# Reordering the start of a fused attention and feed-forward kernel: batch 0 first, a fourth scratch set, a fourth staging place

## The chip, the cores and the metric

The kernel runs on one core of one Trainium2 chip. The metric is the device time of one execution in microseconds (us). Five engines work from queues of their own, each in order: TensorE (PE; its weight loads are listed as PEld), VectorE (DVE), ScalarE (ACT), GpSimd (POOL) and SyncE (SP), which here only issues DMAs.

## The reference, cut to what matters

```python
B, H, S, Ns, D = (4, 8, 512, 32, 64)

def _attn_ref(x, state):                       # x: B,H,S,D   state: B,H,Ns,D
    scale = 1.0 / np.sqrt(D)
    a  = softmax(scale * x @ state.T)          # over the 32 state rows, for each position
    xread = a @ state
    a2 = softmax(scale * state @ x.T)          # over the 512 positions, for each state row
    sread = a2 @ x
    return concat([xread, sread], axis=2)      # B, H, 512 + 32, D

def _moe_ref(x, w_in, w_out, alpha):           # 2176 tokens x 512; d_ff = 2048
    h = x @ w_in
    return (max(h, 0) + alpha * min(h, 0)) @ w_out

def _moe2_ref(x, w_in, w_out):
    h = x @ w_in
    return (max(h, 0) + log1p(exp(-abs(h)))) @ w_out

out = _moe2_ref(_moe_ref(attn as tokens x 512, ...), ...)
```

Both softmaxes subtract their maximum and add 1e-9 to their sum (written out in the code below). The four weight matrices are in double precision; the kernel turns each tile of them into single precision itself.

## The kernel before

The two feed-forward layers are `m = 0` and `m = 1`. Each is cut into four quarters `q` of 512 of the 2048 hidden columns. For each quarter the token blocks 0 to 3 (the 512 positions of a batch) and block `B` (the 128 state rows of all batches) are run through: `hidden` makes the hidden values of 128 columns (`fc`), `act` the activation and its split into a high and a low part (`g0h`, `g0l` and so on), and `out_part`, three jobs later (`LAG`), the second product, added up in `acc`. A block of positions has four jobs, block B has one; `n` counts the jobs of a quarter, 0 to 16. Each product of the layers is three matmuls on split values (`mm3`, L136 to L138): high by high, high by low, low by high.

In the first layer the attention's read is folded into the weights: the hidden value of a position is its softmax (`at`, from the row part of the attention) times the product of state and weights (`sw`, from `sw_batch`, L238). So hidden block 0 of a batch needs `at` and `sw` of this batch, and `sw` of a quarter needs its four tiles of `w_in`.

The attention works in eight groups `i` of four heads, two for each batch. For each group: `x` and `y` load it transposed (`xt`) and plain (`xs`); `s` makes the scores of state rows by positions (L269), copies them to SBUF (L270) and runs the softmax over positions (L271 to L275); `r` transposes the scores (L283) and runs the softmax over state rows (L286 to L292); `b` transposes this back and splits it into `at` (L299, L142, L145); `d` reads with the softmax over positions (L308 to L330) and leaves the state rows' tokens in `sr` for block B. Each group holds a scratch set of six 128x512 places; there are three sets, borrowed from places that are used later, taken in turn by `i % 3`.

A weight tile is loaded (`wload`) into one of three staging places of 4 KB a partition, converted (`wconv`: two ScalarE operations, L202 and L203, three VectorE operations, L204 to L206, and one sum on POOL, L207) and, except for `w_in` of the first layer, split (`wprep`: L142 on ScalarE, L145 on POOL). The intermediate tiles `top` and `exp` exist once. A conversion asks for the next load when it is done. Tiles are converted at most four ahead of what is prepared.

The order of the start is written out by hand: `LOADS` (first DMAs), `BEFORE` (ahead of the first hidden block) and `AMONG` (ahead of job `n` of the first quarter). A letter is a step and its digit the group: `L` load of a weight tile, `p` prepare one (convert it if need be, then split), `c` convert one, `w` the state products of a batch, and the letters above. This is the order of the program; when the kernel is built, a scheduler sets the order on each engine, which may put a later step first where an earlier one is not ready by its own reckoning. PSUM has two pools of four banks, `psa` (state products, hidden blocks, most of the attention) and `psb` (output parts, and some of the first groups).

Of the kernel before, what the change touches and what calls it, by code (L numbers as in the profile page):

```python
# [8 lines left out]
F32 = mybir.dt.float32  # L9
F32R = mybir.dt.float32r  # L10
BF16 = mybir.dt.bfloat16
U16 = mybir.dt.uint16
# [6 lines left out]
P = 128  # L19
# [25 lines left out]

LOADS = "L0 x0 L0 y0 x1 L0 x2 y2 y1"
BEFORE = "p0 s0 c0 s1 r0 p0 c0 r1 d0 b0 p0 x3 d1 y3 p0 w0 b1 p0 y4 s2 p0 r2 c0 x4 s3 w1 c0"
AMONG = ("d2 r3 b2", "d3 s4 x5", "b3", "r4", "s5 y5 p0 d4 x6", "p0 r5 s6", "y6 d5 r6 b4 b5", "", "y7 x7 s7 d6", "b6 r7", "d7 b7")

SPLIT_FIRST = (9, 10, 11, 12, 13, 14, 15, 16)  # L50
SPLIT = (1, 2, 4, 5, 7, 9, 10, 16)
# [7 lines left out]
def mixer_kernel(  # L59
# [26 lines left out]
    class Place:  # L86
# [11 lines left out]
        r = property(lambda self: self.get(F32R))  # L98

    def sbp(name):  # L100
        return Place(name + "h"), Place(name + "l")
# [20 lines left out]
    g_p = pairs(4, "g")  # L122
    acc = [Place(f"acc{i}") for i in range(17)]
    stg = [sbt([P, W], I64, f"stg{i}") for i in range(3)]
    cnv = [sbt([P, W], F32, f"cnv{i}") for i in range(4)]
    tmp = [sbt([P, W], F32, f"tmp{i}") for i in range(3)]
# [5 lines left out]
    st_s = [sbt([P, 16], F32, f"sts{i}") for i in range(2)]  # L132
    st_n = [sbt([P, 2], F32, f"stn{i}") for i in range(3)]

# [46 lines left out]
    def is_whole(i):  # L181
        return wsrc[i][:2] == ("i", 0)

    def wload():
        i = nload[0]
        if i < len(wsrc):
            to, of = stg[i % len(stg)].bitcast(U16), wsrc[i][4].bitcast(U16)
            nc.sync.dma_start(out=to[:, 0 : 4 * W - 1], in_=of[:, 1 : 4 * W])
            nload[0] += 1

    def wconv():

        i = nconv[0]
        if i >= len(wsrc) or i >= nprep[0] + len(cnv):
            return
        s = stg[i % len(stg)]
        top = s.bitcast(U16).rearrange("p (n t) -> p n t", t=4)[:, :, 2]
        low = s.bitcast(U32).rearrange("p (n t) -> p n t", t=2)[:, :, 0]
        a = take_place(i).f if is_whole(i) else cnv[i % len(cnv)]
        t, e = (x[i % len(x)] for x in top_t)  # L200
        tu, eu = t.bitcast(U16), e.bitcast(U16)
        nc.scalar.activation(e, top.bitcast(BF16), AF.Abs)  # L202
        nc.scalar.activation(tu, eu, AF.Relu, bias=top_bias, scale=TOP_SCALE)  # L203
        nc.vector.scalar_tensor_tensor(out=tu, in0=top, scalar=TOP_SIGN, in1=tu, op0=ALU.bitwise_and, op1=ALU.bitwise_or)  # L204
        nc.vector.tensor_scalar(eu, tu, TOP_EXP, None, op0=ALU.bitwise_and)  # L205
        nc.vector.scalar_tensor_tensor(out=a, in0=low, scalar=REST, in1=e, op0=ALU.mult, op1=ALU.mult)  # L206
        nc.gpsimd.tensor_tensor(out=a, in0=t, in1=a, op=ALU.add)  # L207
        wload()
        nconv[0] += 1
# [35 lines left out]
    NG = 2 * B  # L245
    sets = [acc[8:14], flat(wo_p[4:7]), acc[14:17] + [wi_p[4][0], wi_p[4][1], at_p[7][1]]]

    def at_load_t(i):
# [7 lines left out]
    def scratch(i):  # L256
        for x in sets[i % 3]:
            held.pop(x.name, None)
        return [x.f for x in sets[i % 3]]

    def at_scores(i):

        b, g = i // 2, i % 2
        t, n2 = scratch(i), st_n[i % 3]
        ps = bank(pool_s(i))
# [4 lines left out]
        nc.scalar.activation(t[4], ps, AF.Copy)  # L270
        nc.vector.tensor_reduce(out=n2[:, 0:1], in_=ps, op=ALU.max, axis=AX.X)  # L271
        nc.vector.tensor_scalar(n2[:, 0:1], n2[:, 0:1], -SCALE, None, op0=ALU.mult)
        nc.scalar.activation(t[5], ps, AF.Exp, bias=n2[:, 0:1], scale=SCALE, accum_out=n2[:, 1:2])
        nc.vector.tensor_scalar(n2[:, 1:2], n2[:, 1:2], EPS, None, op0=ALU.add)
        nc.vector.reciprocal(n2[:, 1:2], n2[:, 1:2])  # L275

    def at_rows(i):
# [11 lines left out]
        nc.vector.tensor_reduce(out=s1, in_=e3, op=ALU.add, axis=AX.X)  # L289
        nc.vector.tensor_scalar(s1, s1, EPS, None, op0=ALU.add)  # L290
        nc.vector.reciprocal(s1, s1)
# [10 lines left out]
    def at_read(i):  # L302

        b, g = i // 2, i % 2
        t, n2 = scratch(i), st_n[i % 3]
        ps = bank(pool_s(i))
# [145 lines left out]
    def at_do(what):  # L452
        for x in what.split():
            i = int(x[1:])
            if x[0] == "s":
                at_scores(i)
            elif x[0] == "r":
                at_rows(i)
# [29 lines left out]
    for m in range(2):  # L488
        for q in range(NQ):
            first = m == 0 and q == 0  # L490
            blocks = (0, 1, 2, B, 3) if first else (0, 1, B, 2, 3)
            n = 0
            for b in blocks:
                for fc in range(4 if b < B else 1):
# [9 lines left out]
                    todo.append((m, q, b, fc, g))  # L504
                    wconv()
                    if m == 0:
                        if n in SW_AHEAD and q < NQ - 1:
                            sw_batch(q + 1, SW_AHEAD.index(n))
                        if first and b in (0, 1) and fc == 2:
                            sw_batch(q, b + 2)  # L510
                        if not first and n == SW_LAST:
                            sw_batch(q, B - 1)
                    if n in (SPLIT_FIRST if first else SPLIT):
                        wprep()
# [39 lines left out]
```

## Time and profile before

| | us |
|---|---|
| median of 3 runs | 753.28 |
| lowest, highest | 752.79, 753.40 |
| the profiled execution | 752.3 |
| its span, from the first to the last instruction | 750.5 |
| busy: TensorE, VectorE, ScalarE, POOL | 727.6, 425.3, 423.2, 170.5 |
| mean granted clock of TensorE | 0.995 |

Busy TensorE means that a matmul is in its pipeline by the profile's model of its end; neighbouring matmuls overlap, so that busy time is no measure of pace. The granted clock is 1.00 at 2.4 GHz and 0.50 at 1.2 GHz. Idle time in brackets names what ended it.

### The profile page before, as it was taken

The numbers are of one execution on the slowest core, as the hardware profiler recorded it, in microseconds if no ns is written. First come the engines' busy times: TensorE is split into PE (matmuls) and PEld (weight loads), VectorE is DVE, ScalarE is ACT, GpSimd is POOL, SyncE is SP. The second block draws the span as 40 slices with busy tenths as digits, with TensorE's granted clock in tenths as the row PEclk, the third lists the DMA queues.
The fourth block names the chain that finished last, engine by engine and source line by source line (L and its number), as shares of the span: only waits on it lengthen the run. The fifth ranks groups of instructions, "written<-read, shape, count | busy, mean of one in ns | idle before, by whom it ended". The sixth has DMA issues, their size and how long they took to land.

```text
span 750.5 us, 9504 instructions
## 1 busy us (share of the span) xinstructions
PE 727.6 (97%) x3580; PEld 561.7 (75%) x3580; DVE 425.3 (57%) x693; ACT 423.2 (56%) x764; POOL 170.5 (23%) x142
## 2 busy tenths in 40 slices
PE   5699998999999999999999999999999999999998
PEld 2267665777777777878888888888888888888886
DVE  4898657757778447885575224654257342333433
ACT  4778767735554335554677647755466354444560
POOL 2352332402142003452571003410044000000000
PEclk9989999999999999999999999999999999999999
DMA  9654313203211001220122001220010000001102
GB/s 323 221 174 156 107 44 115 85 7 108 83 57 57 0 1 58 86 82 1 56 79 91 0 1 57 84 85 1 0 57 0 1 1 0 1 1 56 57 15 112
DMA packets 16654, 47.27 MB, mean 63 GB/s; under 512 B 2016, under 2 KB 2016, under 8 KB 16608
## 3 DMA queue, kind: packets, MB, share of 16 engines
q1 hardware_dynamic: 16608, 46.66, 18.4%
q8 instruction: 28, 0.46, 0.3%
q14 instruction: 18, 0.15, 0.1%
HBM read 42.20 MB, written 4.46 MB: 62 GB/s over the span
## 4 chain that ended last, share of the span: by engine, by line
PE 94%; DVE 2%; ACT 2%; DMA 1%; issue 1%; POOL 0%; SPq 0%; ACTq 0%
PE pb L136 17%; PE pb L138 17%; PE pb L137 17%; PE pa L136 13%; PE pa L137 12%; PE pa L138 12%; PE pa L238 2%; PE pa L359 2%; PE pa L269 1%; DMA acc<-xt 1%; DVE top L204 1%; PE pa L367 0%; ACT exp L202 0%; PE pb L269 0%; ACT top L203 0%
## 5 line engine op out<-in xcount | busy, mean ns | idle before, releaser
L386 DVE SCALAR_TENSOR_TENSOR pa<-pa,tmp 128x512 f32<-128x512 f32 x68 | 47.4, 697 | 128.8 <-ACT tmp L385 128.8
L383 ACT ACTIVATE tmp<-pa 128x512 f32<-128x512 f32 x68 | 40.5, 596 | 92.7 <-PE pa L138 73.0
L429 DVE TENSOR_TENSOR acc<-pb,acc 128x512 f32<-128x512 f32 x102 | 67.4, 686 | 37.4 <-PE pb L138 37.4
L204 DVE SCALAR_TENSOR_TENSOR top<-stg,top 128x512 uint16<-128x512 uint16 x64 | 53.0, 828 | 46.8 <-ACT top L203 46.2
L207 POOL TENSOR_TENSOR cnv<-top,cnv 128x512 f32<-128x512 bf16 x48 | 56.4, 1175 | 101.0 <-DVE cnv L206 97.2
L379 DVE SCALAR_TENSOR_TENSOR pa<-tmp,rest,pa 128x512 f32<-128x512 f32 (+1 forms) x80 | 53.2, 671 | 25.7 <-ACT tmp L375 25.2
L202 ACT ACTIVATE exp<-stg 128x512 bf16<-128x512 bf16 x64 | 42.9, 671 | 38.7 <-DVE cnv L206 28.6
L375 ACT ACTIVATE tmp<-pa 128x512 f32<-128x512 f32 x68 | 40.2, 596 | 43.0 <-PE pa L138 36.4
L203 ACT ACTIVATE top<-exp,top_bias 128x512 uint16<-128x512 uint16 x64 | 46.1, 721 | 9.2 <-POOL cnv L207 5.5
L385 ACT ACTIVATE tmp<-tmp 128x512 f32<-128x512 f32 x68 | 42.9, 630 | 1.7
L384 ACT ACTIVATE tmp<-tmp 128x512 f32<-128x512 f32 x68 | 42.9, 631 | 1.5
L206 DVE SCALAR_TENSOR_TENSOR cnv<-stg,exp 128x512 f32<-128x512 uint32 x48 | 35.8, 745 | 13.0 <-POOL wo5l L145 4.1
L205 DVE TENSOR_SCALAR exp<-top 128x512 uint16<-128x512 uint16 x64 | 32.1, 502 | 1.1
L142 ACT ACTIVATE g1h<-pa 128x512 fp32r<-128x512 f32 x33 | 19.7, 596 | 20.8 <-DVE pa L386 12.4
L142 ACT ACTIVATE g3h<-pa 128x512 fp32r<-128x512 f32 x33 | 19.7, 596 | 19.3 <-DVE pa L379 9.6
L142 ACT ACTIVATE g0h<-pa 128x512 fp32r<-128x512 f32 x33 | 19.6, 594 | 19.1 <-DVE pa L379 10.2
L145 DVE TENSOR_TENSOR g3l<-pa,g3h 128x512 fp32r<-128x512 f32 x33 | 22.7, 689 | 13.4 <-ACT g3h L142 13.2
L145 DVE TENSOR_TENSOR g1l<-pa,g1h 128x512 fp32r<-128x512 f32 x33 | 22.7, 688 | 12.7 <-ACT g1h L142 12.3
L145 DVE TENSOR_TENSOR g0l<-pa,g0h 128x512 fp32r<-128x512 f32 x33 | 22.7, 688 | 10.5 <-ACT g0h L142 10.1
L145 DVE TENSOR_TENSOR g2l<-pa,g2h 128x512 fp32r<-128x512 f32 x33 | 22.7, 687 | 10.0 <-ACT g2h L142 9.9
L142 ACT ACTIVATE g2h<-pa 128x512 fp32r<-128x512 f32 x33 | 19.7, 597 | 14.5 <-DVE pa L386 7.6
L145 POOL TENSOR_TENSOR wo3l<-cnv,wo3h 128x512 fp32r<-128x512 f32 x5 | 6.5, 1294 | 76.1 <-ACT wo3h L142 75.9
(863 smaller groups left out, 2119.7 us busy)
## 6 DMA issues: line engine op xcount, KB each, us to landing
stg<-w1i SPq DMA_DIRECT2D x16, 511.8 KB, 4.0
stg<-w1o SPq DMA_DIRECT2D x16, 511.8 KB, 3.4
stg<-w2i SPq DMA_DIRECT2D x16, 511.8 KB, 3.9
stg<-w2o SPq DMA_DIRECT2D x16, 511.8 KB, 3.3
out<-acc SPq DMA_DIRECT2D x16, 256.0 KB, 2.0
acc<-xt SPq DMA_DIRECT2D x10, 256.0 KB, 4.8
acc<-xs SPq DMA_DIRECT2D x8, 256.0 KB, 5.3
wo4h<-xt SPq DMA_DIRECT2D x3, 256.0 KB, 3.5
```

Source lines behind the costliest of these rows:

```text
L136: nc.tensor.matmul(ps, lh, rh, start=start, stop=False)
L137: nc.tensor.matmul(ps, lh, rl, start=False, stop=False)
L138: nc.tensor.matmul(ps, ll, rh, start=False, stop=stop)
L142: nc.scalar.activation(h, src, AF.Copy)
L145: eng_l.tensor_tensor(out=l, in0=src, in1=h, op=ALU.subtract)
L202: nc.scalar.activation(e, top.bitcast(BF16), AF.Abs)
L203: nc.scalar.activation(tu, eu, AF.Relu, bias=top_bias, scale=TOP_SCALE)
L204: nc.vector.scalar_tensor_tensor(out=tu, in0=top, scalar=TOP_SIGN, in1=tu, op0=ALU.bitwise_and, op1=ALU.bitwise_or)
L207: nc.gpsimd.tensor_tensor(out=a, in0=t, in1=a, op=ALU.add)
L379: nc.vector.scalar_tensor_tensor(out=ps[:, cs], in0=t[:, cs], scalar=a, in1=ps[:, cs], op0=ALU.mult, op1=ALU.add)
L386: nc.vector.scalar_tensor_tensor(out=ps, in0=ps, scalar=0.0, in1=t, op0=ALU.max, op1=ALU.add)
L429: nc.vector.tensor_tensor(out=a, in0=ps, in1=a, op=ALU.add)
```

## The change

The order lists are written anew: the four `w_in` tiles and both groups of batch 0 go first; other groups, the conversions of `w_out` and batch 1's state products come after them. The position softmax is a step of its own (`e`, `at_positions`), which reads the scores' copy in SBUF in place of PSUM and comes later than the scores. Three operations on one or 16 values a partition go from VectorE to POOL. There are four scratch sets (`i % 4`) and four places for the position softmax's maximum and sum. The fourth weight tile has a staging place of its own, which later holds `acc0` and `acc1` (`Half`). In the first quarter block B comes last, conversions stop at 16 tiles, the state products of batches 2 and 3 move from jobs 2 and 6 to jobs 5 and 9, and one preparation moves from the first quarter to the second (`SPLIT_SECOND`).

```diff
-LOADS = "L0 x0 L0 y0 x1 L0 x2 y2 y1"
-BEFORE = "p0 s0 c0 s1 r0 p0 c0 r1 d0 b0 p0 x3 d1 y3 p0 w0 b1 p0 y4 s2 p0 r2 c0 x4 s3 w1 c0"
-AMONG = ("d2 r3 b2", "d3 s4 x5", "b3", "r4", "s5 y5 p0 d4 x6", "p0 r5 s6", "y6 d5 r6 b4 b5", "", "y7 x7 s7 d6", "b6 r7", "d7 b7")
-SPLIT_FIRST = (9, 10, 11, 12, 13, 14, 15, 16)
+LOADS = "L0 x0 L0 x1 L0 L0 y0"
+BEFORE = "p0 s0 p0 s1 r0 p0 r1 x2 y1 p0 b0 w0 b1 x3 y2 y3"
+AMONG = (
+    "e0 d0 s2 p0", "r2 s3 e1 d1 p0", "r3 b2 p0", "b3 w1 p0 x4 y4",
+    "e2 d2 x5 y5", "s4 r4 e3 d3", "s5 r5 b4 x6 y6", "b5 e4 d4 x7 y7",
+    "e5 d5 s6 r6", "s7 r7 b6 e6", "d6 b7", "e7 d7",
+)
+SPLIT_FIRST = (9, 10, 11, 12, 13, 14, 15)
+SPLIT_SECOND = (2, 3, 4, 5, 7, 9, 10, 12, 16)
...
-    acc = [Place(f"acc{i}") for i in range(17)]
+    acc01 = {"name": "acc01"}
+    acc = [Half(acc01, 0), Half(acc01, 1)] + [Place(f"acc{i}") for i in range(2, 17)]
+    stg_3 = sbt([P, W], I64, acc01["name"])
...
-    st_n = [sbt([P, 2], F32, f"stn{i}") for i in range(3)]
+    st_n = [sbt([P, 2], F32, f"stn{i}") for i in range(4)]
...
+    def stage(i):
+        return stg_3 if i == 3 else stg[(i - (i > 3)) % len(stg)]
...
-        wload()
+        if i != 3:
+            wload()
...
+    sets.append([ex_p[0][1], ex_p[1][0], ex_p[1][1], wi_p[5][0], wi_p[5][1], sr[1]])
...
         nc.scalar.activation(t[4], ps, AF.Copy)
-        nc.vector.tensor_reduce(out=n2[:, 0:1], in_=ps, op=ALU.max, axis=AX.X)
-        nc.vector.tensor_scalar(n2[:, 0:1], n2[:, 0:1], -SCALE, None, op0=ALU.mult)
-        nc.scalar.activation(t[5], ps, AF.Exp, bias=n2[:, 0:1], scale=SCALE, accum_out=n2[:, 1:2])
-        nc.vector.tensor_scalar(n2[:, 1:2], n2[:, 1:2], EPS, None, op0=ALU.add)
+
+    def at_positions(i):
+
+        t, n2 = scratch(i), st_n[i % len(st_n)]
+        nc.vector.tensor_reduce(out=n2[:, 0:1], in_=t[4], op=ALU.max, axis=AX.X)
+        nc.gpsimd.tensor_scalar(n2[:, 0:1], n2[:, 0:1], -SCALE, None, op0=ALU.mult)
+        nc.scalar.activation(t[5], t[4], AF.Exp, bias=n2[:, 0:1], scale=SCALE, accum_out=n2[:, 1:2])
+        nc.gpsimd.tensor_scalar(n2[:, 1:2], n2[:, 1:2], EPS, None, op0=ALU.add)
         nc.vector.reciprocal(n2[:, 1:2], n2[:, 1:2])
...
-        nc.vector.tensor_scalar(s1, s1, EPS, None, op0=ALU.add)
+        nc.gpsimd.tensor_scalar(s1, s1, EPS, None, op0=ALU.add)
...
-            blocks = (0, 1, 2, B, 3) if first else (0, 1, B, 2, 3)
+            blocks = (0, 1, 2, 3, B) if first else (0, 1, B, 2, 3)
...
-                    wconv()
+                    if not first or nconv[0] < 4 * NQ:
+                        wconv()
...
-                        if first and b in (0, 1) and fc == 2:
-                            sw_batch(q, b + 2)
+                        if first and n in (5, 9):
+                            sw_batch(q, 2 + (n == 9))
...
-                    if n in (SPLIT_FIRST if first else SPLIT):
+                    if n in (SPLIT_FIRST if first else SPLIT_SECOND if (m, q) == (0, 1) else SPLIT):
```

## Rows read from the trace of the kernel before

**Rows 1.** The page: busy us (share of the span) and instructions of TensorE.
```profile
PE 727.6 (97%) x3580; PEld 561.7 (75%) x3580; DVE 425.3 (57%) x693; ACT 423.2 (56%) x764; POOL 170.5 (23%) x142
```
**Rows 2.** Windows: stretch, its length, busy by engine, granted clock, DMA share, GB/s.
```profile
7.27:35.42 28.15, 19.88 (x166) 7.40 (x167) 22.65 (x51) 18.96 (x44) 9.71 (x9) 0.98 0.80 291
35.42:41.70 6.28, 6.28 (x50) 3.75 (x50) 6.16 (x14) 4.78 (x11) 3.32 (x3) 0.53 0.37 126
41.70:125.00 83.30, 79.66 (x557) 54.70 (x554) 63.25 (x124) 61.84 (x137) 28.33 (x24) 1.00 0.36 118
...
160.00:200.00 40.00, 40.00 (x193) 29.71 (x192) 30.28 (x54) 21.69 (x36) 8.22 (x7) 1.00 0.29 93
```
**Rows 3.** The chain that ended last: start us, us, engine, tile, line.
```profile
34.69 0.68 DVE sw2l L145
35.44 0.78 PE pa L136
...
42.90 0.23 PE pa L137
...
55.90 0.99 PE pa L269 x8
...
58.26 0.44 PE pa L308 x4
...
70.85 0.58 PE pa L314 x32
...
108.25 3.43 PE pa L359 x8
```
**Rows 4.** Windows of 1 us: length, busy TensorE, granted clock, DMA share, GB/s.
```profile
31.00:32.00 1.00, 0.00 (x0) 1.00 0.82 305
...
35.00:36.00 1.00, 0.58 (x1) 0.50 0.19 41
...
42.00:43.00 1.00, 1.00 (x6) 1.00 0.62 174
```
**Rows 5.** Timeline, end of the first quarter: start, us, instruction [idle before].
```profile
121.49 0.50 PE L136 MATMUL pa<-at6h,sw6h 128*128 128x512 f32 x1 [2.37 <-DVE g1l L145]
```
**Rows 6.** Timeline: fourth weight tile's load and conversion's end, batch 0's last input.
```profile
13.25 0.33 SPq L188 DMA_DIRECT2D stg<-w1i  x1
...
24.75 1.16 POOL L207 TENSOR_TENSOR wi1l<-top,wi1l 128x512 f32<-128x512 bf16 x1 [2.15 <-DVE wi1l L206]
...
30.27 0.69 DVE L145 TENSOR_TENSOR sw1l<-pa,sw1h 128x512 fp32r<-128x512 f32 x1 [0.44 <-ACT sw1h L142]
```
**Rows 7.** Timeline: the first weight tile's conversion.
```profile
6.69 0.72 ACT L203 ACTIVATE top<-exp,top_bias 128x512 uint16<-128x512 uint16 x1
...
7.44 0.69 DVE L204 SCALAR_TENSOR_TENSOR top<-stg,top 128x512 uint16<-128x512 uint16 x1 [6.58 <-ACT top L203]
...
9.27 1.16 POOL L207 TENSOR_TENSOR wi0h<-top,wi0h 128x512 f32<-128x512 bf16 x1 [7.97 <-DVE wi0h L206]
```
**Rows 8.** Timeline: the first and the last of the four output tiles' conversions.
```profile
28.52 1.17 POOL L207 TENSOR_TENSOR cnv<-top,cnv 128x512 f32<-128x512 bf16 x1 [2.61 <-DVE cnv L206]
...
47.79 1.18 POOL L207 TENSOR_TENSOR cnv<-top,cnv 128x512 f32<-128x512 bf16 x1 [1.49 <-DVE cnv L206]
```
**Rows 9.** Timeline: group 7 from its row transposes to `at7l`; block 3's first product.
```profile
92.25 0.60 PE L283 MATMUL pa<-ident,wo6h 128*128 128x128 f32 x4
...
103.67 0.69 DVE L145 TENSOR_TENSOR at7l<-pa,at7h 128x512 fp32r<-128x512 f32 x1 [4.67 <-ACT at7h L142]
...
116.45 0.48 PE L136 MATMUL pa<-at6h,sw6h 128*128 128x512 f32 x1
```
**Rows 10.** Timeline: POOL's nearest small operation; a product and a 16-bit operation beside it.
```profile
1.01 0.29 POOL masks.py:199 TENSOR_SCALAR_AFFINE_SELECT ident<-ident 128x128 f32<-128x128 f32 x1
...
21.54 1.05 POOL L292 TENSOR_TENSOR wo4l<-wo4l,sts 128x512 f32<-128x512 f32 x1 [0.49 <-DVE sts L291]
21.84 1.30 DVE L204 SCALAR_TENSOR_TENSOR top<-stg,top 128x512 uint16<-128x512 uint16 x1 [0.47 <-ACT top L203]
```

More of the change, by code (lines that the diff above doesn't have):

```diff
@@ L98, in mixer_kernel, with __init__, f @@
         r = property(lambda self: self.get(F32R))
+    class Half:
+        def __init__(self, both, k):
+            self.name, self.both, self.k = f"{both['name']}{k}", both, k
+        @property
+        def f(self):
+            if "f" not in self.both:
+                self.both["f"] = sbt([P, 2 * W], F32, self.both["name"])
+            return self.both["f"][:, self.k * W : (self.k + 1) * W]
     def sbp(name):
@@ L186, in wload @@
         if i < len(wsrc):
-            to, of = stg[i % len(stg)].bitcast(U16), wsrc[i][4].bitcast(U16)
+            to, of = stage(i).bitcast(U16), wsrc[i][4].bitcast(U16)
             nc.sync.dma_start(out=to[:, 0 : 4 * W - 1], in_=of[:, 1 : 4 * W])
@@ L195, in wconv @@
             return
-        s = stg[i % len(stg)]
+        s = stage(i)
         top = s.bitcast(U16).rearrange("p (n t) -> p n t", t=4)[:, :, 2]
@@ L256, in scratch @@
     def scratch(i):
-        for x in sets[i % 3]:
+        for x in sets[i % len(sets)]:
             held.pop(x.name, None)
-        return [x.f for x in sets[i % 3]]
+        return [x.f for x in sets[i % len(sets)]]
     def at_scores(i):
         b, g = i // 2, i % 2
-        t, n2 = scratch(i), st_n[i % 3]
+        t = scratch(i)
         ps = bank(pool_s(i))
@@ L304, in at_read @@
         b, g = i // 2, i % 2
-        t, n2 = scratch(i), st_n[i % 3]
+        t, n2 = scratch(i), st_n[i % len(st_n)]
         ps = bank(pool_s(i))
@@ L456, in at_do @@
                 at_scores(i)
+            elif x[0] == "e":
+                at_positions(i)
             elif x[0] == "r":
```

## The prediction

> **What bounds the kernel now.** I read the page first: TensorE is busy 97% of the span [rows 1]. Then the busy time by stage [rows 2]: from 41.7 us on TensorE is nearly full, and in the stretch of 160 to 200 us it is full while VectorE has a quarter and ScalarE almost half of the time free. So no change off TensorE can help there, and only the start is open. TensorE's first matmul is at 7.27 us, when the first transposed group has landed; its first matmul of the feed-forward part (L136) is at 35.42. Between the two it counts as busy for 19.88 of 28.15 us, but a busy TensorE is not TensorE at its pace, so I price the work instead, with the chain's rows at full clock [rows 3]: a set of score or state products (eight 64x512) 0.99, four transposes 0.44, the 32 small products of a read 0.58, one 128x512 product 0.23. Issued in that stretch: scores of four groups 3.96, four row transposes 1.76, two whole reads (0.44 + 0.58 + a quarter of 0.44 = 1.13) 2.26 and the transposes of a third 0.44, two back transposes 0.88, state weights of two batches 3.96: 13.3 us. So 14.9 of the 28.15 us are lost.
>
> After this comes a stretch at the lower clock: the granted clock falls to 0.50, that is 1.2 GHz, after TensorE had done little for some microseconds, and is back at 1.00 (2.4 GHz) by 42 us [rows 4]. From 35.42 to 41.70 it did six products, one set of transposes, the small products of one read and one score set: 1.38 + 0.44 + 0.58 + 0.99 = 3.4 us of work in 6.28, so 2.9 lost. Later there is one visible hole, 2.37 us before 121.49, where a hidden block waits for a PSUM bank that g1l gives free [rows 5]. The losses that the change can reach are thus 14.9 + 2.9 + 2.4 = 20.2 us.
>
> Why does the feed-forward start so late? Batch 0's last input, sw1l, is done at 30.27 + 0.69 = 30.96 [rows 6], and the chain of waits then shows the first hidden block waiting for sw2l, done at 35.37 [rows 3]: that is batch 1's state product, made ahead of hidden block 0, and it held a bank of the pool of four that the hidden blocks use. VectorE is busy 22.65 of the 28.15 us [rows 2], and its queue is in order.
>
> **The change part by part.**
>
> *Loads.* Before, the fourth weight tile is issued at 13.25, since its staging place has to be read first [rows 6]. After, it has a place of its own and goes out with the first three, ahead of x2, y2 and y1; x1 goes ahead of y0. The queue's bytes up to there are nearly the same, so the first matmul stays at 7.27. No cost.
>
> *Weights of batch 0.* The first conversion ends at 9.27 + 1.16 = 10.43 [rows 7]; the fourth ends at 24.75 + 1.16 = 25.91 [rows 6], so the next three take (25.91 - 10.43)/3 = 5.2 each. The bound from below: the next tile's L203 must wait until POOL has read `top`, so a period is L203 0.72, then VectorE's three from 7.44 until POOL starts at 9.27 (1.83), then POOL 1.16, and two hops of about 0.05: 3.8. What lies between 3.8 and 5.2 is other work on ScalarE and VectorE: the position softmax of groups 0 and 1 (moved to e0, e1), and s2, r2 and batch 1's part, which the new order puts behind. Four tiles then end between 10.43 + 3 x 3.8 = 21.8 and 25.9; I take 23.9, the middle, because the row softmax of groups 0 and 1 still shares the engines. The last state products (half a set, 0.5), the copy (0.6), the subtraction (0.69) and hops and queue waits of 1.3 follow: batch 0 is ready at 27 (24.5 to 31).
>
> *Work before that.* Of TensorE's work, scores of groups 0 to 3 (groups 2 and 3 wait on no earlier group now that there are four scratch sets), three row transposes, two back transposes, one state batch and one read fit ahead: 3.96 + 1.32 + 0.88 + 1.98 + 1.13 = 9.3 us. Lost: 27 - 7.27 - 9.3 = 10.4 instead of 14.9, **gain 4.4** (0 if batch 0 is no earlier than 31, 6.9 at 24.5). Hidden block 0 no longer stands behind batch 1's state product, and a score bank is free after its copy, because the position softmax reads the copy in SBUF.
>
> *Low clock.* TensorE will again have a sparse stretch before 27 us, but with more work in it. Before, the fall came only after the nearly empty stretch up to 35. I take half: **gain 1.4** (0 to 2.9).
>
> *Feeding it after 27 us.* The output weights come one by one: before, the four tiles are converted from 29.69 to 48.97, 6.4 us apart [rows 8]. After, TensorE has from 27 us hidden blocks 0 to 3 (24 products, 5.5), their output parts (48 products, 11.0) and s4, r3, b2, b3, d1, w1 (5.4): 21.9 us. If the first output tile is done at 28, the others 5.2 apart, and the fourth split 2.5 later, it is ready at 46: 19 us for 21.9 us of work. In sum there is enough; but each queue is in order, so some waits will show: **loss 1.5** (0, up to 3 x (6.4 - 2.8) = 10.8 if nothing stands between the output parts of 2.8 us each).
>
> *Conversions capped at 16 in the first quarter*, where 20 fitted: 4 x 1.8 = 7 us of VectorE go to the second quarter and lie under TensorE there (9.7 us free of 40 [rows 2]). Without that cover it would be up to 7 us. The one preparation more in the second quarter has the same cover.
>
> *State rows' block last.* Its work is the same, so nothing by itself. It takes distance from batch 3: group 7's row transposes at 92.25 lead to at7l at 104.36, and block 3 starts at 116.45 [rows 9], 12.1 us of slack. The state block (3.43 [rows 3], 0.44 and 12 x 0.23: 6.6) and one place (18 x 0.23 = 4.1) go: 1.4 us remain. On the other side the 2.37 us hole came where the state block, batch 3 and two state products shared four banks. I take half of it: **gain 1.2** (from 2.4 to a loss of 2).
>
> *Small operations to POOL*, three a group, 24 in all. No row has one there; the nearest is 0.29 for 128x128 [rows 10], the far bounds nothing and the 1.05 of a 512-wide product. VectorE is spared 24 x 0.15 = 3.6. On batch 0's path lies the one in the row softmax, hidden under the weights' chain, which ends later; without this cover it is 0.3 plus a wait behind one POOL operation, 1.2. I take 0. But VectorE's 16-bit L204 takes 1.30 instead of 0.69 while POOL's product runs from 21.54 to 22.59 [rows 7, 10].
>
> The Trainium skill, "SBUF — State Buffer", section "Who interferes with whom", says that the two engines share one port pair, which whichever starts first holds for the whole instruction while the other is blocked. The trace's 1.30 against 0.69 agrees. By that rule each moved operation is a new hold on VectorE, and the sum would be about 1.8 us worse; by the rows alone it is not.
>
> Sum: -4.4 - 1.4 + 1.5 - 1.2 = -5.5. The profiled execution took 752.3 (span 750.5 and 1.8 around it), so 746.8 on its own scale; the median shown is 1.0 higher, so **747.8 us**.
>
> **The rivals.**
>
> *All of it is kept.* Batch 0 at 24.5, full clock throughout, no waits: -6.9 - 2.9 - 2.4 = -12.2, 741.1. For it: the arithmetic of 21.9 us of work against 19. Against: VectorE near full up to 41.7. Chance 0.17 for below 744.
>
> *Blocked VectorE.* Six moved operations come before 27 us (one each in r0 and r1, two each in e0 and e1), each holding VectorE for 0.3: batch 0 at 28.8, 749.6. The 1.30 row speaks for it, 0.15 spared per operation against. Chance 0.10.
>
> *No earlier.* The order on each engine is made when the kernel is built; if it puts s2, s3 and r2 in front of batch 0's work on VectorE, or banks run out again, batch 0 stays at 31 and the first output tiles are as late as before: 752 to 754. Chance 0.18. The change would then not do what it says.
>
> *Slower: output parts wait in TensorE's queue.* Place: between hidden block 3 and batch 1's hidden blocks. If tiles still come 6.4 us apart and output parts stand in line ahead of everything else, 10.8 is lost against 7.0 gained: 756.6 + 1.0 = 757.1 or so on the median's scale. It decides from 2.3 us of wait per tile, a period of 5.1. For it: before, the period was 6.4 with VectorE full; against: before, TensorE found other work. Chance 0.15.
>
> **How the numbers follow.** The forecast's own case, 744 to 751.5, has 0.40. A measurement of this kernel tells about 0.2% (1.5 us) from no change. Faster: 0.40 + 0.17 + 0.10 = 0.67; within 0.2%: 0.18; slower: 0.15. The range runs from 741.5 (under it 0.02) to 755 (over it 0.15).
>
> **What would show it.** Right: L136's first matmul at 25 to 28 us, its waits there naming sw1l and not sw2l; the fourth weight tile converted by 24; the first score of group 3 before 22; less than 2.9 us lost at clock 0.50; TensorE full between 30 and 48; no wait before batch 3's blocks. Wrong: first L136 past 30; waits of TensorE on output tiles (wo1 to wo3) of over 2 us each between 30 and 48; a wait on at7 or at6 at batch 3; or L204 and L205 often above 1 us.

## The result, and the profile after

The changed kernel takes 758.6 us (median of six runs, 756.28 to 759.72), the kernel before, run beside it, 753.22 (751.86 to 753.83): ratio 1.0071, interval 1.0055 to 1.0087. It is slower by 5.4 us where 5.5 less was forecast, and outside the range. The profiled execution took 756.28, the lowest of the six, so profiles show 4.0 of it.

First the page's busy time, then the windows that answer to those of before; the last two lines are windows from 40 us.

```profile
PE 729.2 (97%) x3580; PEld 562.8 (75%) x3580; DVE 424.0 (56%) x669; ACT 424.7 (56%) x764; POOL 177.1 (23%) x166
```
```profile
7.27:35.42 28.15, 22.92 (x159) 10.63 (x156) 22.45 (x44) 19.58 (x41) 12.97 (x19) 0.94 0.80 297
35.42:41.70 6.28, 3.66 (x15) 2.82 (x14) 6.28 (x13) 4.85 (x14) 3.58 (x5) 0.83 0.73 217
41.70:125.00 83.30, 76.31 (x582) 50.78 (x581) 52.79 (x92) 57.09 (x126) 26.68 (x32) 0.99 0.28 89
...
40.00:60.00 20.00, 18.04 (x92) 12.54 (x90) 12.60 (x21) 12.11 (x22) 8.49 (x8) 0.93 0.44 137
60.00:105.00 45.00, 39.97 (x334) 27.24 (x335) 33.42 (x62) 34.11 (x79) 18.46 (x25) 1.00 0.33 106
```

Against [rows 2], TensorE is busier up to 35.42 (22.92 for 19.88 us), but from there to 125 it is busy 3.66 + 76.31 = 79.97 us where before it was 6.28 + 79.66 = 85.94. VectorE is not short from 41.70 on: 52.79 for 63.25. The kernel before, in the same windows from 40 us:

```profile
40.00:60.00 20.00, 20.00 (x142) 12.44 (x134) 19.20 (x35) 14.64 (x35) 8.92 (x8) 0.97 0.58 185
60.00:105.00 45.00, 43.73 (x351) 30.87 (x349) 31.58 (x66) 33.03 (x77) 13.85 (x12) 1.00 0.32 106
```

TensorE's queue waits for answers more often: 9 waits from 20 to 140 us, 13.1 us in sum, where before there were 7 with 10.0, and only two of those behind 40 us. First the waits after the change, from 20 to 140 us, then the two of before from 40 to 140 us (who waits, for whom, us in total, times, longest):

```profile
PE pb L327 <- POOL acc L320: 2.6, 1, 2.6
PE pa L311 <- ACT wi5l L294: 2.4, 1, 2.4
PE pa L261 <- POOL wi1l L229: 2.2, 1, 2.2
PE pb L155 <- ACT g3h L161: 1.9, 1, 1.9
PE pa L155 <- DVE acc L315: 1.4, 1, 1.4
PE pa L342 <- ACT wo6h L337: 1.2, 1, 1.2
...
```
```profile
PE pa L136 <- DVE g1l L145: 2.4, 1, 2.4
PE pa L136 <- ACT srh L330: 1.2, 1, 1.2
```

L327 is the back transpose of group 2, L311 the row transposes of group 7, L155 a 128x512 product, L342 the small products of a read. The tiles wo6h, wi4l and wi5l in these waits are places that the groups borrow as scratch, not weights. From the timeline, in order: the start of e0 on VectorE, the last step of the fourth weight tile's conversion, the first hidden product, the last step of the first and of the last output tile's conversion, and the output part that waits for g3h.

```profile
9.97 0.69 DVE L299 TENSOR_REDUCE stn<-acc 128x1 f32<-128x512 f32 x1 [1.02 <-ACT acc L294]
...
24.23 1.16 POOL L229 TENSOR_TENSOR wi1l<-top,wi1l 128x512 f32<-128x512 bf16 x1
...
27.44 0.80 PE L155 MATMUL pa<-at0h,sw0h 128*128 128x512 f32 x1
...
29.24 1.17 POOL L229 TENSOR_TENSOR cnv<-top,cnv 128x512 f32<-128x512 bf16 x1 [1.19 <-DVE cnv L228]
...
46.82 1.17 POOL L229 TENSOR_TENSOR cnv<-top,cnv 128x512 f32<-128x512 bf16 x1 [1.68 <-DVE cnv L228]
...
54.76 1.20 PE L155 MATMUL pb<-g3h,wo3h 128*128 128x512 f32 x4 [1.90 <-ACT g3h L161]
```

The start did what was forecast: batch 0's hidden product at 27.44 instead of 35.42 [rows 3]. To see what became of it I priced all of TensorE's work up to an instant at the prediction's prices (the 128x512 product by 0.2275, a quarter of a transpose set by 0.109, a matmul of the state block's L387 by 3.43 / 8 = 0.4286). An instant less the work started by then is an estimate of what TensorE has **lost** by it, in us; the last columns are runs told of below.

```
instant  before  after   e13    e14    e11    e12
  7.27     7.1    7.0    7.0    7.0    7.0    7.0
 27.44    17.5   18.5   19.0   17.8   18.9   17.8
 35.42    22.2   21.5   21.5   22.2   21.8   21.1
 50       26.1   25.2   25.4   27.1   22.7   23.2
 80       27.7   30.0   31.9   30.5   29.2   24.5
105       28.9   34.9   33.0   32.7   32.3   25.8
130       32.3   35.9   33.5   36.9   32.9   29.5
735       28.9   33.0   30.9   34.6   30.2   26.6
```

The changed kernel is 1.0 behind at 27.44, ahead by only 0.7 at 35.42 and 0.9 at 50, loses 3.2 more than before from 50 to 80, 3.7 more from 80 to 105, gains 2.4 from 105 to 130 and gives 0.5 back behind it: +4.1, the difference of the two profiles.

### The profile page after: what moved, and what is told of

It reads as the page before. It is cut to its first block, busy times and chain, and to the rows that moved or that the text cites. A ratio compares the mean times of both kernels' runs of the same rounds, so it can differ in the third digit from the quotient of the medians.

```text
span 754.5 us, 9484 instructions
## 1 busy us (share of the span) xinstructions
PE 729.2 (97%) x3580; PEld 562.8 (75%) x3580; DVE 424.0 (56%) x669; ACT 424.7 (56%) x764; POOL 177.1 (23%) x166
## 4 chain that ended last, share of the span: by engine, by line
PE 90%; DVE 3%; ACT 3%; POOL 1%; issue 1%; DMA 1%; SPq 0%
PE pb L155 16%; PE pb L156 16%; PE pb L157 16%; PE pa L155 12%; PE pa L157 12%; PE pa L156 12%; PE pa L261 3%; PE pa L387 2%; DVE top L226 1%; ACT top L225 1%; DMA acc<-xt 1%; POOL cnv L229 0%; PE pa L395 0%; PE pa L311 0%; PE pb L293 0%
## 5 line engine op out<-in xcount | busy, mean ns | idle before, releaser
L226 DVE SCALAR_TENSOR_TENSOR top<-stg,top 128x512 uint16<-128x512 uint16 x63 | 52.6, 834 | 51.9 <-ACT top L225 51.4
L164 DVE TENSOR_TENSOR g3l<-pa,g3h 128x512 fp32r<-128x512 f32 x33 | 22.7, 689 | 12.8 <-ACT g3h L161 12.5
L164 DVE TENSOR_TENSOR g0l<-pa,g0h 128x512 fp32r<-128x512 f32 x33 | 22.7, 688 | 10.8 <-ACT g0h L161 10.4
L164 DVE TENSOR_TENSOR g2l<-pa,g2h 128x512 fp32r<-128x512 f32 x33 | 22.7, 688 | 10.2 <-ACT g2h L161 10.0
L164 DVE TENSOR_TENSOR g1l<-pa,g1h 128x512 fp32r<-128x512 f32 x33 | 22.7, 687 | 10.3 <-ACT g1h L161 9.9
```

Of the source, the lines that this page charges most:

```text
L164: eng_l.tensor_tensor(out=l, in0=src, in1=h, op=ALU.subtract)
```

## The experiments

Each ratio is to runs of the kernel before on the same chip. e1 to e4 ran on one chip, e5 to e8 on a second, e9 to e12 on a third, e13 to e16 on a fourth; e17 and e18 stand beside runs of their own.

**First ideas: the steps on POOL, the block order, the places, batch 1.**

e1_small_on_vector:
```diff
-nc.gpsimd.tensor_scalar(n2[:, 0:1], n2[:, 0:1], -SCALE, None, op0=ALU.mult)
+nc.vector.tensor_scalar(n2[:, 0:1], n2[:, 0:1], -SCALE, None, op0=ALU.mult)
...
-nc.gpsimd.tensor_scalar(s1, s1, EPS, None, op0=ALU.add)
+nc.vector.tensor_scalar(s1, s1, EPS, None, op0=ALU.add)
```


> The changed kernel with its three small operations a group back on VectorE; all else as changed. Theory 'late batch 1' (the order puts batch 1's steps behind block 0, so that TensorE runs out of work between 50 and 65 us): VectorE gets 3.6 us back and POOL's hops go, but block 1 still starts near 60; 757 to 759. Theory 'POOL' (the small operations wait behind POOL's long ones and lengthen each row softmax): the hole before b2 (2.6 us at 36.7) and those at 83 to 95 us shrink, 753 to 755.

759.51 us, 1.0092 (1.0077 to 1.0107): no gain. The operations on POOL are not the cause.

e2_state_block_fourth:
```diff
-blocks = (0, 1, 2, 3, B) if first else (0, 1, B, 2, 3)
+blocks = (0, 1, 2, B, 3) if first else (0, 1, B, 2, 3)
```


> The changed kernel with the state rows' block back between blocks 2 and 3 of the first quarter; all else as changed. Theory 'late batch 1': the loss lies before 65 us and at 92, where nothing changes; 757 to 760. Theory 'state block' (its place costs the slack of the last groups): 754 to 756, with the hole before 95.0 gone or moved.

762.08 us, 1.0124 (1.0109 to 1.0139): the state block's place last saves about 0.5%, some 4 us, in the changed kernel.

e3_before_with_places (the kernel before with the fourth places and one more early weight load):
```diff
-LOADS = "L0 x0 L0 y0 x1 L0 x2 y2 y1"
+LOADS = "L0 x0 L0 y0 x1 L0 L0 x2 y2 y1"
...
+    sets.append([ex_p[0][1], ex_p[1][0], ex_p[1][1], wi_p[5][0], wi_p[5][1], sr[1]])
...
+    def stage(i):
+        return stg_3 if i == 3 else stg[(i - (i > 3)) % len(stg)]
```


> The kernel before with the new places alone: four scratch sets, the fourth staging place (one more load among the first), four places for maximum and sum; its order lists, its position softmax, its conversions and its block order unchanged. Theory 'late batch 1' (the order costs, the places do not): no slower than before, 751 to 754. Theory 'places' (more loads at once and other borrowed places cost): 755 or more.

755.78 us, 1.0043 (1.0026 to 1.006): there the places cost 3 us. e10 below shows that they are not what the changed order pays for.

e4_batch1_ahead:
```diff
-BEFORE = "p0 s0 p0 s1 r0 p0 r1 x2 y1 p0 b0 w0 b1 x3 y2 y3"
+BEFORE = "p0 s0 p0 s1 r0 p0 r1 x2 y1 p0 b0 w0 b1 x3 y2 y3 s2 r2 s3 w1"
 AMONG = (
-    "e0 d0 s2 p0", "r2 s3 e1 d1 p0", "r3 b2 p0", "b3 w1 p0 x4 y4",
+    "e0 d0 r3 b2 p0", "e1 d1 b3 p0", "p0", "p0 x4 y4",
```


> The changed kernel with batch 1's steps moved forward: s2 r2 s3 w1 to the end of BEFORE, r3 b2 to job 0 and b3 to job 1; all else as changed. Theory 'late batch 1': block 0 starts some us later than 27, but block 1 starts before 57 and the loss between 40 and 65 us shrinks from 8 to about 4; 752 to 755. Theories 'POOL' and 'state block': no better than the changed kernel, 757 to 760.

758.07 us, 1.0069 (1.0054 to 1.0084): the same as the changed kernel. The edit did not bring block 1 forward: it starts at 61.0 (60.72 without the edit), while block 0's first hidden product falls back to 31.6. The wait of group 2's back transposes shrinks from 2.6 to 1.2 and that for g3h goes, so batch 1's steps gain by it what the start loses. Moving them is no gain in sum; what they cost where the change has them stays open. The run also shows that 4 us of the earlier start can be given up without a loss.

**Conversions and queue order.**

e5_two_intermediates, and e8_before_two_intermediates with the same edit on the kernel before:
```diff
+    pair2 = sbt([P, 2 * W], BF16, "acc4")
...
         t, e = (x[i % len(x)] for x in top_t)
+        if i % 2 and i < 10:
+            t, e = pair2[:, 0:W], pair2[:, W : 2 * W]
```


> The changed kernel, with a second pair of the two intermediate tiles for every other output tile among the first ten. In the changed kernel's trace the output tiles' conversions end 5.9 us apart on average between 29.24 and 46.82 us, VectorE is busy for only 17.18 of the 24.58 us from 35.42 to 60, and its output weights are whole only at about 50 us. Conversion-chain theory: one pair of intermediates makes the tiles' steps on POOL, ScalarE and VectorE follow each other, and this sets the pace from 27 to 50 us; with two pairs the tiles come 4 to 5 us apart, the last of the first four some 4 us earlier, block 1 starts by 58 (60.72 now), and the time falls by 2 to 4 us, to 752 to 756. Queue-order theory: what is lost, is lost because steps stand too close behind each other in TensorE's queue; the tiles may come earlier, but the time stays within 1 us of the changed kernel's 756 to 760.

> The kernel before with the same second pair of intermediate tiles for every other output tile among the first ten, as a control. There VectorE is busy for 23.66 of the 24.58 us from 35.42 to 60, so a second pair has no idle VectorE to use. Conversion-chain theory: no gain here, 752 to 754.5. Queue-order theory: the same. Were it to gain as much as in the changed kernel, the pair would help whatever the order, and the chain would not be what the change brought out.

e5: 761.04 us, 1.0109 (1.009 to 1.0129). e8: 755.05, 1.0026 (1.001 to 1.0042). The fourth output tile's POOL step does start at 41.3 instead of 46.82, as the chain theory says, but the time rises: group 2's back transposes now wait longer, as e5's waits of TensorE show.

```profile
PE pb L330 <- POOL acc L323: 4.0, 1, 4.0
PE pb L156 <- ACT g3h L162: 3.1, 1, 3.1
...
```

So an earlier arrival of the tiles alone gains nothing. That the faster tiles' steps stand ahead of the softmax and the activations in VectorE's and ScalarE's queues is read from these waits; no run shows it apart.

e6_scores_earlier:
```diff
-    "e2 d2 x5 y5", "s4 r4 e3 d3", "s5 r5 b4 x6 y6", "b5 e4 d4 x7 y7",
-    "e5 d5 s6 r6", "s7 r7 b6 e6", "d6 b7", "e7 d7",
+    "e2 d2 s4 x5 y5", "r4 e3 d3 s5", "r5 b4 x6 y6", "b5 e4 d4 s6 x7 y7",
+    "e5 d5 r6 s7", "r7 b6 e6", "d6 b7", "e7 d7",
```


> The changed kernel with the scores of groups 4 to 7 one job earlier, so that each stands a whole job of hidden products ahead of the row transposes that need its softmax. In the changed kernel's trace TensorE stands for 2.4 us from 92.65 to 95.04 at group 7's row transposes, directly behind its scores, and about 5 us more are lost than in the kernel before between 50 and 105 us. Queue-order theory: that hole goes, and others at the row transposes with it: 1.5 to 3 us less, 753.5 to 757 where the changed kernel has about 758. Conversion-chain theory: what is not done in one hole is waited for at the next, since the weights of the next block come no earlier: within 1 us of the changed kernel.

757.1 us, 1.006 (1.0041 to 1.0079), inside the changed kernel's interval. The wait of 2.4 at group 7's row transposes goes; an output part waits 3.3 for g0h at 94.67 instead. The scores alone, one job earlier, move a hole.

e7_output_tiles_ahead:
```diff
-BEFORE = "p0 s0 p0 s1 r0 p0 r1 x2 y1 p0 b0 w0 b1 x3 y2 y3"
+BEFORE = "p0 s0 p0 s1 r0 p0 r1 x2 y1 p0 c0 b0 w0 b1 c0 x3 y2 y3"
```


> The changed kernel with two of the output weights' conversions placed ahead of batch 0's hidden products and of its last weights (the steps of the other conversions follow as before). Conversion-chain theory: the output weights are whole some 4 to 6 us earlier, and so is the first read of block 0; batch 0's own weights come later by the conversions put ahead of them, some 2 to 3 us of VectorE; the time falls by 0 to 2 us. Queue-order theory: the start of block 0 is later by what is put ahead of it and nothing is won behind it: the same or up to 2 us slower than the changed kernel.

756.82 us, 1.0055 (1.0037 to 1.0072): not to be told from the changed kernel.

e9_positions_with_scores:
```diff
-nc.vector.tensor_reduce(out=n2[:, 0:1], in_=t[4], op=ALU.max, axis=AX.X)
+nc.vector.tensor_reduce(out=n2[:, 0:1], in_=ps, op=ALU.max, axis=AX.X)
...
 def at_positions(i):
+    pass
```


> The changed kernel with the position softmax of each group undone to where the kernel before has it: directly behind the group's scores, read from PSUM, its three small steps on VectorE. Theory A (the late position softmax brings the loss between 50 and 105 us, since ScalarE and VectorE get it together with the row softmax of the next groups): 753 to 756 us where the changed kernel has about 758, and the part lost from 50 to 105 us falls from about 10 toward the 3 us of the kernel before. Theory B (the loss comes from what TensorE is left with once block 0's hidden products are done early, wherever the position softmax stands): 757 to 760.

759.49 us, 1.0093 (1.0078 to 1.0108): no gain, so the later position softmax is not the cause. In the changed kernel's trace e0's reduction ran at 9.97 us in any case, since the order on each engine is made when the kernel is built.

e10_batch0_first_three_places:
```diff
-    sets.append([ex_p[0][1], ex_p[1][0], ex_p[1][1], wi_p[5][0], wi_p[5][1], sr[1]])
...
-LOADS = "L0 x0 L0 x1 L0 L0 y0"
-BEFORE = "p0 s0 p0 s1 r0 p0 r1 x2 y1 p0 b0 w0 b1 x3 y2 y3"
+LOADS = "L0 x0 L0 x1 L0 y0"
+BEFORE = "p0 s0 p0 s1 r0 p0 r1 x2 y1 p0 b0 w0 b1 y2"
...
-    "e0 d0 s2 p0", "r2 s3 e1 d1 p0", "r3 b2 p0", "b3 w1 p0 x4 y4",
+    "e0 d0 x3 y3 s2 p0", "r2 s3 e1 d1 x4 y4 p0", "r3 b2 p0", "b3 w1 p0",
```


> The changed kernel's order without the fourth set of places and without the fourth staging place: batch 0 first, three sets, the fourth weight tile loaded when the first place is free, and loads of groups 3, 4 and 6 moved behind the reads that free their set. The fourth places alone, put into the kernel before, took 3.0 us more (755.78 to 752.79). Theory A (the places themselves bring the loss, by the transfers that they let start early): 754 to 757 and no later hole for want of a group. Theory B (the order brings it, and the places soften it): 759 to 764, the first hidden product 1 to 3 us later than 27.4, and new waits of the scores of groups 3 and 4 for their loads.

757.41 us, 1.0066 (1.0051 to 1.0081): the same as with the fourth places, its first hidden product even at 24.87. Both theories missed: the changed order is as slow without the places as with them, and a hidden product 2.6 us earlier gains nothing. What the places cost in e3 stays open.

e11_output_weights_light, and e12_before_output_weights_light with the same edit on the kernel before:
```diff
+        if 4 <= i < 8:
+            nc.scalar.activation(a, top.bitcast(BF16), AF.Copy)
+            wload()
+            nconv[0] += 1
+            return
         t, e = (x[i % len(x)] for x in top_t)
```


> The changed kernel with the conversion of the first four output weight tiles cut to one ScalarE copy of their top 16 bits (left out: the other ScalarE, VectorE and POOL steps of tiles 4 to 7, and so the values of those weights; the splits that follow stay). Theory A, the supply of output weights sets TensorE's pace from 27 to 55 us: the changed kernel gets its early start back, loses 4 to 5 us less by 60 us, and takes 752 to 755 us. Theory B, what TensorE lacks there is the attention of batches 1 to 3, whose softmax steps follow each other: it loses at most 2 us less, and takes 756 to 759.

> The kernel before with the same cut (left out: the same steps of tiles 4 to 7 and the values of those weights), as a control. VectorE is busy there for 23.66 of the 24.58 us from 35.42 to 60, so it gets back 4 times about 2.3 us of VectorE. Theory A (supply of output weights): it gains too, 1 to 4 us, 749 to 752, but less than the changed kernel. Theory B (attention): the gain goes to the attention's VectorE steps and is about the same size, or larger than in the changed kernel, whose VectorE idles.

e11: 753.13 us, 1.0004 (0.9994 to 1.0014). e12: 750.57, 0.9969 (0.9958 to 0.998). Without these conversions both gain, about 5.0 (1.0071 less 1.0004) and 2.5 us (750.57 for 753.08), so these conversions, by their work or by when their tiles are whole, are a real load on both orders, on the changed one more. But from 50 to 105 us e11 still loses 9.6 (32.3 - 22.7) and e12 2.6. That part is something else.

**Groups 4 to 7.** By 60 us VectorE had been busy for 39.75 us in the changed kernel and 46.38 before, ScalarE for 38.57 and 40.54; most of VectorE's difference lies between 40 and 60 (12.60 and 19.20). The changed order issues the scores of group 4 at the sixth job, the one before at the second.

e13_next_groups_earlier:
```diff
-    "e0 d0 s2 p0", "r2 s3 e1 d1 p0", "r3 b2 p0", "b3 w1 p0 x4 y4",
-    "e2 d2 x5 y5", "s4 r4 e3 d3", "s5 r5 b4 x6 y6", "b5 e4 d4 x7 y7",
-    "e5 d5 s6 r6", "s7 r7 b6 e6", "d6 b7", "e7 d7",
+    "e0 d0 s2 p0 x4 y4", "r2 s3 e1 d1 p0 x5 y5", "r3 b2 p0 s4", "b3 w1 p0 r4",
+    "e2 d2 s5 x6 y6", "e3 d3 r5 x7 y7", "b4 s6 e4 d4", "b5 r6",
+    "e5 d5 s7", "r7 b6 e6", "d6 b7", "e7 d7",
```


> The changed kernel with the loads, scores and row softmax of groups 4 to 7 one to two jobs earlier. In the changed kernel VectorE is busy for only 13.3 us from 40 to 60 us (44.2 less 30.9 done by then) where the kernel before has 21.1 less a rounding (all 20), and the scores of group 4 stand ahead of block 1's second hidden product at 64.6, where the kernel before has them ahead of block 0's second at 41.7. Late-groups theory: the work comes into the idle stretch, the part lost from 50 to 105 us falls from 10 to about 5, and the time to 752 to 755. Contention theory (conversions of the next weights stand in the way): no gain, 757 to 760.

e14_before_groups_later:
```diff
-AMONG = ("d2 r3 b2", "d3 s4 x5", "b3", "r4", "s5 y5 p0 d4 x6", "p0 r5 s6", "y6 d5 r6 b4 b5", "", "y7 x7 s7 d6", "b6 r7", "d7 b7")
+AMONG = ("d2 r3 b2", "d3 x5", "b3", "", "y5 p0 x6", "s4 r4 p0", "y6 s5 d4 r5 b4", "b5 x7", "y7 d5 s6 r6", "s7 d6 r7 b6", "b7", "d7")
```


> The kernel before with the scores of groups 4 to 7 put where the changed kernel has them (group 4 at the sixth job instead of the second, group 5 at the seventh instead of the fifth, and so on), all else as before. Late-groups theory: it loses 3 to 6 us more from 50 to 105 us and takes 756 to 759. Contention theory: within 1.5 us of 753.

e13 moves the scores of groups 4 to 7 by one to three jobs, with loads and row softmaxes; e14 moves row softmaxes and reads along with the scores, but hardly the loads (only x7), so the loads are not what counts there.

e13: 753.66 us, 1.0004 (0.9994 to 1.0014). e14: 758.04, 1.0053 (1.0035 to 1.0071). The late groups alone carry the kernel before about as far as the whole change did; with these groups earlier, the changed kernel's slowdown is gone. e13's waits of TensorE from 20 to 140 us, its window from 60 to 105, and of e14 some of the waits that the kernel before has not:

```profile
PE pa L261 <- POOL wi1l L229: 2.2, 1, 2.2
PE pa L342 <- ACT wi4l L337: 1.9, 1, 1.9
PE pa L155 <- DVE sw2l L164: 1.8, 1, 1.8
PE pb L342 <- ACT wi5l L337: 1.5, 1, 1.5
PE pa L155 <- DVE acc L315: 1.4, 1, 1.4
PE pb L327 <- POOL acc L320: 0.3, 1, 0.3
```
```profile
60.00:105.00 45.00, 43.47 (x367) 28.89 (x359) 32.79 (x58) 33.50 (x78) 18.69 (x22) 0.96 0.37 118
```
```profile
...
PE pa L314 <- ACT acc L309: 1.8, 1, 1.8
PE pa L283 <- ACT wo6h L270: 1.4, 1, 1.4
...
PE pb L299 <- POOL wo4l L292: 0.8, 1, 0.8
...
PE pa L299 <- POOL acc L292: 0.6, 1, 0.6
```

In e13 the wait of group 2's back transposes shrinks from 2.6 to 0.3, that of group 7's row transposes (2.4) is gone, and TensorE is busy 43.47 of the 45 us instead of 39.97. From 80 to 105 us it loses 1.1 (33.0 - 31.9), like the kernel before (1.2), where the changed one loses 4.9. In e14 the row transposes (L283) wait for the copy of their scores and the back transposes (L299) for their softmax, as they do in the changed kernel.

The times bear out the late groups in both directions; the place does so in part. From 50 to 105 us e13 still loses 7.6 (33.0 - 25.4, about 5 forecast), since what it saves from 80 to 105 it had partly lost before: TensorE waits 1.9 before 59.68, and the granted clock is then 0.50 from 60 to 63 (0.96 in the window above). Profiles show 2.0 of the gain of e13 over the changed kernel, its medians 5. e14's loss of 5.7 is spread over all stretches: 1.0 up to 50 us, 1.8 from 50 to 80, 1.1 from 80 to 105 and the rest behind.

e15_second_weights_light, and e16_before_second_weights_light (the edit of e11, for tiles 8 to 15, in either order):
```diff
+        if 8 <= i < 16:
+            nc.scalar.activation(a, top.bitcast(BF16), AF.Copy)
```


> The changed kernel with the conversions of weight tiles 8 to 15 (the second quarter's) cut to one ScalarE copy of their top 16 bits (left out: the other ScalarE, VectorE and POOL steps of those tiles and the values of those weights). They run from 52 to 88 us in the changed kernel. Contention theory: attention and activations get ScalarE and VectorE to themselves there, the part lost from 50 to 105 us falls from 10 to 3 to 5, the time to 751 to 754. Late-groups theory: it falls by 2 at most, 756 to 758.

> The kernel before with the same cut of weight tiles 8 to 15 (left out: the same steps and values), as a control: 55 to 92 us there. Contention theory: it gains 0 to 2 us, since only 3 are lost from 50 to 105. Late-groups theory: the same. A gain as large as in the changed kernel would mean that the cut shortens what both share.

e15: 761.29 us, 1.0101 (1.0085 to 1.0118). e16: 753.28, 1.0001 (0.9989 to 1.0013). No gain in either, but e15 does more than spare ScalarE and VectorE work. Its timeline of ScalarE, and the product that waits for it:

```profile
52.23 0.68 ACT L223 ACTIVATE cnv<-stg 128x512 f32<-128x512 bf16 x1 [1.12 <-DMA stg<-w1o]
...
58.69 0.58 ACT L408 ACTIVATE tmp<-pa 128x512 f32<-128x512 f32 x1
...
60.74 1.22 PE L155 MATMUL pb<-g3h,wo3h 128*128 128x512 f32 x2 [7.54 <-ACT g3h L161]
```

The short conversions run into the weight loads, ScalarE stands at them, and the activation of block 0's fourth product (L408) stands behind: TensorE waits 7.54 us for g3h. What speaks against contention with these conversions as the main cause is e13 and e14, not this run.

**Two attempts to get below the kernel before**, both on e13: e17_groups_earlier_w1 (the first pair of lines) and e18_groups_earlier_c0 (the second).
```diff
-"r2 s3 e1 d1 p0 x5 y5", "r3 b2 p0 s4", "b3 w1 p0 r4"
+"r2 s3 w1 e1 d1 p0 x5 y5", "r3 b2 p0 s4", "b3 p0 r4"
...
-p0 b0 w0 b1 x3 y2 y3
+p0 c0 b0 w0 b1 c0 x3 y2 y3
```


> The changed kernel with groups 4 to 7 earlier, and with the product w1 of batch 1 two jobs earlier, ahead of block 0's second hidden product. In the run with groups 4 to 7 earlier, block 0's fourth hidden product (42.52 us) waits 1.8 us for VectorE to have taken w1's sums out of PSUM. If this wait is real, it goes: 751 to 753.5, faster than the kernel before by up to 0.3%. If another wait takes its place (the output weights are whole no earlier, at about 50 us): 753 to 756.

> The changed kernel with groups 4 to 7 earlier, and with two of the output weights' conversions issued ahead of batch 0's hidden products (alone, in the changed kernel, this gave 756.82 for 758.1). If the two edits add up: 752 to 753. If the output weights' supply is the bound up to 50 us whatever stands around it, 752.5 to 754.5, the same as the kernel before.

e17: 755.66 us, 1.0034 (1.0021 to 1.0048). e18: 756.17, 1.0043 (1.003 to 1.0055). Both are slower than the kernel before, and above e13's 1.0004, so an edit of one or two steps can cost over 2 us here. No version that does all the work beats the kernel before.

## Why the prediction was wrong

**The start.** It came out nearly as forecast: the hidden product at 27.44 (27), lost by then 18.5 - 7.0 = 11.5 (10.4), and 22.2 - 7.1 = 15.1 before by 35.42 (14.9), so 3.6 of "**gain 4.4**". The instant was met partly by luck. The fourth weight tile ended at 24.23 + 1.16 = 25.39, not at 23.9, hardly earlier than the 25.91 of before; from there to the hidden product it took 2.05 instead of the 3.1 in the sum. What this gain is worth rests wholly on TensorE keeping its pace behind 27 us: by 27.44 the kernel before had lost only 10.4 (17.5 - 7.1) itself, with other work done in that time, and at 35.42 no more than 0.7 of the gain is left.

**Feeding it after 27 us.** This is the first step that failed: "In sum there is enough ... **loss 1.5**" was mis-sized, and its window was too short. From 27.44 to 50 the changed kernel loses 6.7 (25.2 - 18.5), of which about 2.7 is the low clock of the next paragraph, so some 4.0 instead of 1.5. No wait names an output tile. TensorE stands for VectorE and POOL in the row softmax of batch 1 (1.4 at L155, 2.6 at L327) while VectorE is busy for all of 35.42 to 41.70. Counting the work that "fits" said nothing of when it is ready.

**Low clock.** Forecast was a gain of 1.4. Windows of 1 us of the changed kernel (length, busy by engine, granted clock):

```profile
26.00:27.00 1.00, 1.00 (x12) 0.14 (x11) 0.53 (x1) 1.00 (x3) 0.00 (x0) 0.50 0.07 20
27.00:28.00 1.00, 1.00 (x15) 0.77 (x13) 1.00 (x4) 0.90 (x2) 0.16 (x1) 0.50 0.00 0
28.00:29.00 1.00, 1.00 (x4) 0.63 (x3) 1.00 (x2) 0.91 (x3) 0.05 (x1) 0.50 0.28 80
...
38.00:39.00 1.00, 0.00 (x0) 0.00 (x0) 1.00 (x3) 0.98 (x3) 1.00 (x1) 1.00 0.88 317
39.00:40.00 1.00, 0.66 (x5) 0.66 (x5) 1.00 (x4) 0.68 (x2) 0.29 (x1) 0.79 0.95 356
40.00:41.00 1.00, 1.00 (x5) 0.81 (x4) 1.00 (x3) 0.60 (x1) 0.27 (x1) 0.50 0.23 84
41.00:42.00 1.00, 1.00 (x4) 0.81 (x3) 1.00 (x3) 0.33 (x1) 0.28 (x1) 0.50 0.66 111
42.00:43.00 1.00, 1.00 (x3) 0.78 (x3) 0.40 (x2) 0.43 (x2) 1.00 (x2) 0.50 0.56 186
```

It is granted 1.2 GHz twice, each time after a wait (2.21 us before 25.45, 2.62 before 39.34): six whole windows at 0.50, each half lost, 3.0 us, and 0.4 in the windows around them. By the same estimate the one fall of before cost 3.4 as well (2.9 by the prediction's count from 35.42 on). No gain. Up to 50 us the three steps together were to give -4.4 - 1.4 + 1.5 = -4.3; they gave -0.9.

**What the sum left out.** This is the step that cost most. From 50 to 105 us no term stood for the late groups, nor a reason for putting them at nothing, and there 6.9 were lost on top of before. The steps of groups 4 to 7, moved behind batch 0, were counted as work that stands somewhere else, not as answers that somebody waits for. The prediction's own remark that "each queue is in order, so some waits will show" was applied to the output tiles alone. e13 and e14, with times that move by 4 to 5 us either way, show that this order of the groups is what made the change slow; the waits that go in e13 account for most of the 3.7 lost from 80 to 105. Of the 3.2 lost from 50 to 80 the mechanism is not settled: in e13 that stretch is worse (31.9 - 25.4 = 6.5, for the changed kernel's 4.8), with reads waiting for ScalarE's copies of their transposes (1.9 and 1.5) where in the changed kernel an output part waited for g3h.

**State rows' block last.** Right in sign and cause: 1.2 forecast; the hole of [rows 5] is gone, no wait stands before batch 3, 2.4 is gained from 105 to 130 and 0.5 given back later; in e2 a wait of 2.33 stands before batch 3 again (131.62), and some 4 us are lost. **Conversions capped at 16**: no loss shows behind 130 us beyond that 0.5. **Small operations to POOL**: nothing, as forecast; one of 128x16 took 0.27 us at 35.90 and 0.36 on average. By the prediction's reading of the port rule of the Trainium skill ("SBUF — State Buffer", "Who interferes with whom") they would have cost about 1.8. That reading was too wide: the section lets VectorE contend only in its two-port modes or with two inputs in SBUF, not in every instruction. e1 gave nothing back, and L226, the operation that rose to 1.30 beside POOL's product [rows 10], took 864 ns on average up to 130 us after the change and 905 in e1, where the small operations are back on VectorE. The rule itself is not refuted; no run here shows a price of it for operations this small.

**The rivals.** The slower one had the sign. Its place, between hidden block 3 and batch 1's hidden blocks, does have a wait, but of 1.9 us and for ScalarE's g3h, not for output tiles; their period was 5.9 (29.24 to 46.82), above its 5.1, without the 10.8 it priced. (Its sum should read 756.1 + 1.0 = 757.1. The forecast's own period of 5.2 already lay above the 5.1 from which this rival decides.) e11 shows that the output tiles' conversions cost the changed kernel 5 us; e5, where the tiles come earlier and the time rises, speaks against their arrival as the way. "All of it is kept" failed with the two falls of the clock and the waits behind 27 us, "Blocked VectorE" with e1, "No earlier" with the first hidden product. The main cause, late groups, was none of the rivals.

## What to carry to other kernels

Compare an earlier start at the same instant, by work done, not by the time of one instruction: whatever the engine did instead in the old order was work too, and the lead lasts only as long as the engine keeps its pace. When a batch is put first, ask what is put second, and list for each step that moves back who needs its answer and how long the chain to it is; an engine with an in-order queue waits there, however idle the others are. A pair of runs that moves the same steps in both orders, earlier in one and later in the other, says more on such a cause than single undo runs: here it gave 4 to 5 us each way, as forecast, while single edits that were to gain cost 2 us and more (e5, e17, e18).

## What was not expected of the hardware

A wait of TensorE can cost more than its length: after 2.62 us without work the granted clock was 0.50 for three windows, another 1.5 us and more, in a stretch that had work again. Not every wait does: behind the 2.38 us before 95.04 it stayed at 1.00. And the kernel is touchy: a second pair of intermediates (e8, +2.4 us by the medians) or places that the old order does not need (e3, +3.0) made the kernel before slower, though neither adds an instruction to TensorE.
